# Two one-element GpSimd copies ahead of block 1's first weight sums, in a linear-attention and leaky-ReLU MLP kernel

## The chip, the core and the metric

The kernel runs on one core of one Trainium2 chip. Its time is the device time of one execution in microseconds (us). Five engines work side by side, each through its own queue of instructions in order: TensorE (PE in the profile; PEld is its weight load), VectorE (DVE), ScalarE (ACT), GpSimd (POOL) and SyncE (SP), which here only issues transfers. Engines wait for each other by semaphores.

## What is computed

Attention without softmax, with a root-mean-square norm, feeds a two-layer MLP. In float32, except that `w_in` and `w_out` reach the kernel as float64:

```python
kv = einsum('bhsd,bhse->bhde', k, v)          # batch 8, heads 8, seq 576, head 64
out = einsum('bhsd,bhde->bhse', q, kv)
x = out / sqrt(mean(out * out, -1) + 1e-6) * g_norm   # -> 4608 x 512
h = x @ w_in                                  # 512 x 2048
y = maximum(0.01 * h, h) @ w_out              # 2048 x 512
```

## The kernel before

The 4608 rows of `x` are cut into nine blocks of 512 (block 0 to 8). The 2048 columns between the two layers are cut into four chunks (`c`), each of two halves (`h`) of two tiles (`u`) of 128: sixteen tiles.

**Weights.** `w_in` and `w_out` come as 32 transfers of 64-bit numbers ("jobs"), one `w_in` and one `w_out` piece for each tile. The raw bits land in one of seven places in turn (three parts of `stage`, four of `pairs`, L209). Each job is rounded to float32 by two ScalarE instructions (L245, L247) and four VectorE instructions (L249 TENSOR_SCALAR, L253 TENSOR_SCALAR, L255 SCALAR_TENSOR_TENSOR, L258, a custom one), the last of which completes the weights. The jobs are paired crosswise (L269), so the last two are the `w_out` pieces of tile 14 and tile 15, both halves of the tile `w2_sb[1][3]`.

**Block 0** (`first_block`, L1037) runs while the weights still come. For tile n, TensorE makes `h_ps` (tile n of the hidden layer), ScalarE applies the leaky ReLU (L1055, `g`), and then TensorE adds tile n-1's product with `w_out` to four accumulators (`o_acc`). In float32 each written matmul shows as two in the trace, so both steps are groups of 8. Between the steps, `between` (L1081) loads and rounds jobs and runs block 1's attention in small steps. At the end the accumulators are copied out (L1069 ScalarE, L1071 VectorE).

**Blocks 1 to 8** use Strassen's seven products in the order 1, 2, 6, 5, 7, 3, 4 (and from block 2 a second level). For these the weights must be added up first:

- `sides_w1(c)` (L640): four GpSimd sums over a chunk of `w_in`. `sides[5]` and `sides[6]` go to `pair(0)`, `sides[7]` and `sides[3]` to `pair(1)` (`pair(i)` is the i-th quarter of `pairs`). `sides[6]` is made from `sides[5]`, `sides[3]` from `sides[6]`.
- `sides_w2(0)` (L662): four GpSimd sums over `w_out`, written to `pair(2)` and `pair(3)`.
- `combine(0, part)` (L702): eight GpSimd sums for parts 0 and 1, from `pair(0)` and `pair(1)` to `stage`, and transfers of both to DRAM by SyncE (L725 to L727), for the second level.
- `sides_x(1)` (L752): VectorE sums of block 1's `x` (`xt`, `xT`).

All such sums run through one helper, L636. An instruction that is not pinned (`pin`, L90) may be moved by the scheduler, which keeps dependences between overlapping pieces of a tile. In the built program of the kernel before, GpSimd's first sums stand as: `sides[7]`, the four sums of `w_out`, `sides[5]`, `sides[6]`, `sides[3]`, then the eight of `combine`. `sides[5]` must wait until ScalarE has read the last raw job, since that lies in `pair(0)`.

VectorE's instructions at that place stand as: the rounding of the jobs, where the last two alternate and tile 14's half is completed last; two sums for block 1's norm (L418); `xt`, `xt`, `xT` (L636); two transposes (L455); two copies of `o_acc` (L1071); a last `xt`; and `g<-h_c`, the first accumulation of block 1. TensorE's `o_acc` group of tile 14 waits for VectorE's completion of tile 14's half and for ScalarE's `g` of tile 14; the group of tile 15 waits for `g` of tile 15. The fourth product group of block 1 (product 5) waits for `g<-h_c`, which frees its bank.

Of the kernel before, what the change touches and what calls it, by code (L numbers as in the profile page):

```python
# [23 lines left out]
def kernel(  # L24
# [36 lines left out]
    nc = tc.nc  # L61
    B, H, S, D = q.shape
    DM, DF = w_in.shape
    P = 128
# [8 lines left out]
    U = 2  # L73
    NC = DF // 2 // (U * P)
# [30 lines left out]
    def view(t, lo, *shape):  # L105
        n = 1
        for d in shape:
            n *= d
        t = t[:, lo:lo + n]
        names = "abcd"[:len(shape)]  # L110
        return t.rearrange(f"p ({' '.join(names)}) -> p {' '.join(names)}",
                           **dict(zip(names, shape))) if len(shape) > 1 else t

    def pair(i, *shape):
        return view(pairs, i * NW, *shape)
# [74 lines left out]
    def make_ident():  # L190
# [9 lines left out]
    w2_sb = [[consts.tile([P, U, DM], F32, name=f"w2_{h}_{c}") for c in range(NC)]  # L200
             for h in range(2)]
# [433 lines left out]
    def add(eng, out_, a, b_, minus=False, pinned=False):  # L635
        ins = eng.tensor_tensor(out_, a, b_, op=ALU.subtract if minus else ALU.add)  # L636
        if pinned or steady:
            pin(ins)

    def sides_w1(c):  # L640


        a11, a12 = w1_sb[0][c][:, :, :2, :], w1_sb[0][c][:, :, 2:, :]
        a21, a22 = w1_sb[1][c][:, :, :2, :], w1_sb[1][c][:, :, 2:, :]
        s12 = pair(0, U, 2, 2, P)
        sides = {1: a11, 2: a12, 4: a22, 5: s12[:, :, :, 0, :], 6: s12[:, :, :, 1, :]}
        add(nc.gpsimd, sides[5], a21, a22)
        add(nc.gpsimd, sides[6], sides[5], a11, True)

        def more():  # L650
            s34 = pair(1, U, 2, 2, P)
            sides.update({7: s34[:, :, :, 0, :], 3: s34[:, :, :, 1, :]})
            add(nc.gpsimd, sides[7], a11, a21, True)
            add(nc.gpsimd, sides[3], a12, sides[6], True)
        return sides, more
# [443 lines left out]
    x_sides, _, sums, _ = sides_x(1)  # L1099
    for _ in sums:  # L1100
        pass
    h_sides, more = sides_w1(0)
    more()
    for part in range(2):
# [148 lines left out]
```

## Time and profile before

| | us |
|---|---|
| median of four runs | 917.39 (917.07 to 917.91) |
| the profiled execution | 917.91 |
| its span | 915.4 |
| outside the span | 2.5 |
| TensorE busy | 908.7 (99%) |
| VectorE busy | 634.7 (69%) |
| GpSimd busy | 367.4 (40%) |
| ScalarE busy | 327.7 (36%) |

A timeline line reads: start, duration of the group, engine, source line, operation, output<-input, partitions x elements, count; in brackets the idle time of the engine before it and what the profile takes to have ended it. All times are from the start of the span. The granted TensorE clock is 1.0 in every stretch of this profile.

### The profile page before, as it was taken

How to read it: one execution, taken by the hardware profiler on the slowest of the kernel's cores; microseconds unless marked ns; L12 is line 12 of the kernel's file. 1: busy time of each engine (PE TensorE's matmuls, PEld its weight loads, DVE VectorE, ACT ScalarE, POOL GpSimd, SP SyncE). 2: the span in 40 equal slices, each digit the busy share in tenths (PEclk: the TensorE clock that was granted, in tenths of full speed). 3: DMA queues.
4: the chain of work that ended last, by engine and by line, in shares of the span. 5: the costliest groups of instructions: out<-in, count | busy, mean ns of one | idle time of the engine just before them, and what ended most of it. 6: DMA issues, size and time to landing. Idle time of an engine off the chain costs nothing.

```text
span 915.4 us, 18027 instructions
## 1 busy us (share of the span) xinstructions
PE 908.7 (99%) x6976; PEld 775.8 (85%) x6976; DVE 634.7 (69%) x1168; ACT 327.7 (36%) x645; POOL 367.4 (40%) x438
## 2 busy tenths in 40 slices
PE   8999999999999999999999999999999999999998
PEld 5444448888998999899999999999999999999997
DVE  5876995587457876587756786678659755755565
ACT  5454433242135233533343324332343333223330
POOL 2000255977633472226321642264226422642222
PEclk9999999999999999999999999999999999999999
DMA  8999916885598779776986689757755666567632
GB/s 266 226 241 240 265 65 217 275 291 167 179 381 262 224 209 271 230 231 215 258 256 217 219 249 271 223 177 226 230 181 177 188 221 201 184 187 224 196 109 92
DMA packets 90228, 200.05 MB, mean 219 GB/s; under 512 B 9888, under 2 KB 42272, under 8 KB 90144
## 3 DMA queue, kind: packets, MB, share of 16 engines
q1 hardware_dynamic: 79680, 187.04, 68.6%
q10 hardware_dynamic: 10016, 10.69, 3.4%
q8 instruction: 55, 0.90, 0.4%
q0 software_dynamic: 448, 1.18, 0.3%
q14 instruction: 29, 0.24, 0.1%
HBM read 172.39 MB, written 26.48 MB: 217 GB/s over the span
## 4 chain that ended last, share of the span: by engine, by line
PE 96%; DVE 1%; DMA 1%; ACT 0%; issue 0%; POOL 0%; ACTq 0%; DVEq 0%; POOLq 0%
PE o_a L118 19%; PE o_c L118 18%; PE h_ha L118 11%; PE h_hb L118 11%; PE h_hc L118 8%; PE h_hd L118 8%; PE o_acc L118 6%; PE h_ps L118 6%; PE o_ps L118 3%; PE h_a L118 2%; PE h_b L118 2%; PE h_c L118 1%; PE h_d L118 1%; PE kv_ps L118 1%; DMA pairs<-in_v_dram 1%; DVE g L636 1%
## 5 line engine op out<-in xcount | busy, mean ns | idle before, releaser
L636 POOL TENSOR_TENSOR gs<-g 128x512 f32<-128x512 f32 x64 | 81.7, 1276 | 252.9 <-ACT g L832 250.9
L832 ACT ACTIVATE g<-g 128x512 f32<-128x512 f32 x124 | 78.2, 631 | 131.0 <-DVE g L636 131.0
L951 ACT COPY w_all<-h_ha 128x512 f32<-128x512 f32 x84 | 48.8, 582 | 173.9 <-PE h_ha L118 160.4
L118 PE MATMUL o_a<-pairs,gs 128*128 128x256 f32 x384 | 91.3, 381 | 0.0
L118 PE MATMUL o_c<-pairs,gs 128*128 128x256 f32 x376 | 89.2, 380 | 0.0
L636 DVE TENSOR_TENSOR o<-h_hb,o 128x128 f32<-128x128 f32 x104 | 29.8, 286 | 83.3 <-ACT pairs L951 83.2
L636 DVE TENSOR_TENSOR o<-o_c,o 128x512 f32<-128x512 f32 (+1 forms) x91 | 61.1, 672 | 23.9 <-PE o_c L118 23.6
L118 PEld LDWEIGHTS o_a<-pairs,gs 128*128 128x128 f32 x384 | 69.8, 190 | 9.2 <-POOL pairs L636 1.2
L118 PEld LDWEIGHTS o_c<-pairs,gs 128*128 128x128 f32 x376 | 68.3, 190 | 7.6
L636 DVE TENSOR_TENSOR o<-o_a,o 128x512 f32<-128x512 f32 x75 | 51.2, 683 | 28.2 <-PE o_a L118 28.1
L118 PE MATMUL h_ha<-stage,w_all 128*128 128x128 f32 x448 | 59.6, 276 | 0.0
L118 PEld LDWEIGHTS h_ha<-stage,w_all 128*128 128x128 f32 x448 | 56.6, 192 | 3.0 <-issue 0.7
L118 PE MATMUL o_acc<-w,g 128*128 128x512 f32 x128 | 57.8, 595 | 0.7 <-ACT g L1055 0.7
L118 PE MATMUL h_ps<-xT,w_all 128*128 128x512 f32 (+1 forms) x136 | 58.1, 571 | 0.3 <-DVE w_all L258 0.3
L636 POOL TENSOR_TENSOR pairs<-w_all 128x512 f32<-128x512 f32 x8 | 10.6, 1329 | 118.0 <-DMA stage<-in_moe_w_in_dram 91.3
L636 DVE TENSOR_TENSOR g<-g,pairs 128x512 f32<-128x512 f32 x84 | 55.6, 689 | 1.9
L636 POOL TENSOR_TENSOR pairs<-g 128x128 f32<-128x128 f32 x52 | 23.7, 456 | 77.3 <-PE h_hb L118 48.5
L118 PEld LDWEIGHTS o_acc<-w,g 128*128 128x128 f32 x128 | 24.0, 190 | 31.2 <-issue 29.4
L118 PEld LDWEIGHTS h_ps<-xT,w_all 128*128 128x128 f32 x136 | 25.4, 190 | 29.0 <-issue 26.3
L636 DVE TENSOR_TENSOR w_all<-h_hc,w_all 128x512 f32<-128x512 f32 x56 | 38.3, 684 | 15.9 <-PE h_hc L118 15.8
L636 DVE TENSOR_TENSOR o<-h_hd,o 128x128 f32<-128x128 f32 x78 | 22.1, 283 | 38.2 <-ACT pairs L951 38.1
L118 PE MATMUL h_hb<-stage,w_all 128*128 128x128 f32 x336 | 46.7, 275 | 0.0
(228 smaller groups left out, 2264.2 us busy)
## 6 DMA issues: line engine op xcount, KB each, us to landing
w_all<-w SPq DMA_DIRECT2D x196, 448.0 KB, 4.2
pairs<-w SPq DMA_DIRECT2D x56, 512.0 KB, 4.3
out_dram<-o ACTq DMA_DIRECT2D x35, 256.0 KB, 4.7
v_in<-in_v_dram SPq DMA_DIRECT2D x29, 288.0 KB, 5.1
k_in<-in_k_dram SPq DMA_DIRECT2D x28, 288.0 KB, 4.7
q_in<-in_q_dram SPq DMA_DIRECT2D x56, 144.0 KB, 6.3
q_in<-in_q_dram SPq DMA_DIRECT2D x56, 140.0 KB, 6.2
w<-stage SPq DMA_DIRECT2D x12, 512.0 KB, 4.4
```

Source lines behind the costliest of these rows:

```text
L118: pin(nc.tensor.matmul(*args, **kw))
L636: ins = eng.tensor_tensor(out_, a, b_, op=ALU.subtract if minus else ALU.add)
L832: nc.scalar.activation(t, t if src is None else src, func=AF.Prelu, alpha=SLOPE)
L951: nc.scalar.copy(q[:, at], bank)
```

## The change

Between the sums of `x` and `sides_w1(0)`, two GpSimd copies of one element are written:

```diff
     for _ in sums:
         pass
+    for i, r in ((1, 0), (0, 1)):
+        nc.gpsimd.tensor_copy(pair(i, U, 2, 2, P)[:1, 0, 0, r, :1], w2_sb[1][NC - 1][:1, U - 1, :1])
     h_sides, more = sides_w1(0)
     more()
     for part in range(2):
```

Each reads one element of `w2_sb[1][3][:, 1]`, the `w_out` piece of tile 15, which VectorE completes as the last but one. The first writes into the place of `sides[7]`, the second into that of `sides[6]`; those sums overwrite the element, so they come after the copy. In the built program GpSimd's order is then: the four sums of `w_out`, `sides[5]`, the two copies (the first of which waits for VectorE's completion of job 31, tile 15), `sides[6]`, `sides[7]`, `sides[3]`, the eight of `combine`. The order of the instructions on the other four engines is the same as before.

## The prediction

> **What bounds the kernel now.** I read the page's chain by engine first, then TensorE's timeline round the end of block 0, then VectorE's and GpSimd's for the same microseconds. The chain is TensorE nearly everywhere:
>
> ```profile
> PE 96%; DVE 1%; DMA 1%; ACT 0%; issue 0%; POOL 0%; ACTq 0%; DVEq 0%; POOLq 0%
> ```
>
> So only a stretch in which TensorE itself stands still can be shortened. TensorE's timeline shows one at the end of block 0:
>
> ```profile
> 122.73 3.60 PE L118 MATMUL h_ps<-xT,w_all 128*128 128x512 f32 x8
> 126.16 3.60 PE L118 MATMUL o_acc<-w,g 128*128 128x512 f32 x8
> 129.59 3.60 PE L118 MATMUL h_ps<-xT,w_all 128*128 128x512 f32 x8
> 133.91 7.10 PE L118 MATMUL o_acc<-w,g 128*128 128x512 f32 x16 [0.72 <-ACT g L1055]
> 140.85 1.89 PE L118 MATMUL h_a<-xT,w_all 128*128 128x256 f32 x8
> ```
>
> Groups of 8 start 3.43 apart (122.73, 126.16, 129.59). The next should start at 129.59 + 3.43 = 133.02; it starts at 133.91, 0.89 late. Its 16 should take 6.86; they take 140.85 - 133.91 = 6.94. Together block 1's first matmul is 0.97 later than in an unbroken stream. (The printed 0.72 counts idle time from the modelled end of the last matmul, and so less.)
>
> The bracket blames ScalarE's `g` of tile 15, which ended at 133.83. But the group that starts here is tile 14's, whose `g` ended at 126.96. What else it waits for is VectorE's half of `w2_sb[1][3]` for tile 14. Here is VectorE, a rounding undisturbed and then the last three:
>
> ```profile
> 91.61 0.42 DVE L249 TENSOR_SCALAR cut<-cut 128x512 f32<-128x512 f32 x1
> 92.06 0.43 DVE L253 TENSOR_SCALAR w<-cut 128x512 uint32<-128x512 uint32 x1
> 92.53 0.69 DVE L255 SCALAR_TENSOR_TENSOR w<-cut,w 128x512 uint32<-128x512 uint32 x1
> 93.25 0.69 DVE L258 CUSTOM_DVE_ANT_0 w<-w,add 128x1024 uint16<-128x1024 uint16 x1
> ...
> 122.92 1.49 DVE L249 TENSOR_SCALAR cut<-cut 128x512 f32<-128x512 f32 x1
> 124.34 1.75 DVE L258 CUSTOM_DVE_ANT_0 w_all<-w_all,add 128x1024 uint16<-128x1024 uint16 x1
> 126.01 1.49 DVE L249 TENSOR_SCALAR cut<-cut 128x512 f32<-128x512 f32 x1
> 127.42 1.81 DVE L253 TENSOR_SCALAR w<-cut 128x512 uint32<-128x512 uint32 x2
> 129.15 2.34 DVE L255 SCALAR_TENSOR_TENSOR w<-cut,w 128x512 uint32<-128x512 uint32 x2
> 131.42 2.34 DVE L258 CUSTOM_DVE_ANT_0 w<-w,add 128x1024 uint16<-128x1024 uint16 x2
> 133.68 1.54 DVE L418 TENSOR_TENSOR sum<-sq 128x128 f32<-128x128 f32 x2
> ```
>
> The last L258 ends at 131.42 + 2.34 = 133.76; TensorE loads its weights at 133.88. That fits VectorE as the releaser. And VectorE is slow there: L249 takes 1.49 instead of 0.42, L258 1.75 instead of 0.69. GpSimd's timeline says what is beside it:
>
> ```profile
> 122.43 1.70 POOL L636 TENSOR_TENSOR pairs<-w_all 128x512 f32<-128x512 f32 x1 [9.72 <-ACT cut L245]
> 124.21 1.33 POOL L636 TENSOR_TENSOR pairs<-pairs,w_all 128x512 f32<-128x512 f32 x1
> 125.62 1.60 POOL L636 TENSOR_TENSOR pairs<-w_all,pairs 128x512 f32<-128x512 f32 x1
> 127.17 1.78 POOL L636 TENSOR_TENSOR stage<-pairs 128x256 f32<-128x256 f32 x2
> ...
> 134.30 0.77 POOL L636 TENSOR_TENSOR stage<-pairs,stage 128x256 f32<-128x256 f32 x1
> 148.00 1.27 POOL L636 TENSOR_TENSOR pairs<-w_all 128x512 f32<-128x512 f32 x1 [12.93 <-PE h_c L118]
> ```
>
> GpSimd adds without a break from 122.43 to 135.07, just while VectorE is slow, and then idles 12.93 until TensorE frees the next place.
>
> **What the change removes.** Every sum after `sides[5]` now starts only when tile 15's half is rounded. VectorE up to the L258 at 124.34 stays as it is (`sides[5]` still runs beside it, to 124.13). From there I set undisturbed steps, from start to start in the first four lines: L249 0.45, L253 0.47, L255 0.72, L258 0.61 (93.25 to the next L249 at 93.86). So 124.34 + 0.61 + 0.45 + 2 x 0.47 + 2 x 0.72 = 127.78 is the start of tile 15's L258; it ends at 128.47 and lets GpSimd go. Tile 14's L258 starts at 128.39. Undisturbed it ends at 129.08; if the first released sum strikes it, it takes 1.75 and ends at 130.14. TensorE wants it at 133.02, its weights 0.43 earlier at 132.59. Even the later end leaves 2.4. The wait goes whole.
>
> What is late next? Tile 14's `g` (126.96) is early. Tile 15's `g` ends at 133.83 and is wanted at 133.02 + 3.43 = 136.45. So block 1 starts 0.97 earlier, and from there TensorE runs on.
>
> **What it adds.** The two copies: no row shows a GpSimd copy. The nearest are its MEMSET of 128x1, 0.10, and its sum of 128x128, 0.46. A wait can't earn time in itself, so the bounds are 0.2 and 0.9 for both; I take 0.2, since the MEMSET is as small. They lie on GpSimd alone.
>
> **What it moves on GpSimd.** Behind the waiting copy stand `sides[6]`, `sides[7]`, `sides[3]` and eight sums of `combine`. From 128.47, with copies up to 0.92, three sums at 1.33 to 1.70 and the eight at the 7.90 they took (127.17 to 135.07), GpSimd is done at 128.47 + 0.2 + 4.0 + 7.9 = 140.6, at most 142.4. Who waits?
> - TensorE wants `sides[6]` for product 6 at 144.30 - 0.97 = 143.33; it is there by 131.1. `sides[7]` and `sides[3]` come after it (products 7 and 3, at 149.06 and 150.89 in the trace before) and are there by 134.5.
> - GpSimd's own next sums wait for TensorE until 148.00 - 0.97 = 147.03. The idle 12.93 covers the delay of 5.5 to 7.3.
> - SyncE's queue stands behind these sums: the `combine` writes at 125.56 to 133.08 slide by some 6. But its next write waited anyway until 142.07, for a landing of block 0's output, and later ones for VectorE (146.75). The next loads in the queue go out at 154.04. I cost this at nothing; if the cover fails, those loads are late, with 14 us before TensorE's next `kv_ps` at 168.25.
> - `sides[7]` leaves 97.70, where it stretched an L258 to 1.75. VectorE gains 1.06 there and then waits for ScalarE at 104.51 anyway; TensorE has no wait there. Nothing.
>
> **What it moves on VectorE.** After the rounding, VectorE meets the delayed sums. From 130.14: two sums at 0.77 as now beside GpSimd; three `xt`/`xT` at 1.17, the mean of the eight `xT<-xT` rows; two transposes 2.17. That gives 130.14 + 1.54 + 3.51 + 2.17 = 137.4, earlier than now (139.24). The copies of `o_acc` then wait for TensorE, and the last `xt` is done long before `g<-h_c`. Nothing lost.
>
> The trace shows both kinds of VectorE work beside GpSimd: `xT<-xT`, read from SBUF alone, 1.17 instead of 0.68; `o<-o_c,o`, one input in PSUM, 0.68 either way. The Trainium skill, SBUF — State Buffer, section Who interferes with whom, is stricter than the first: an operation with two SBUF inputs is blocked for the whole of a GpSimd operation that reads SBUF. This speaks against the change, which only shifts the blocking from the rounding to the `xt` sums. By that rule the five sums would each wait out one GpSimd sum (an estimate: three of 1.33, two of 0.73), so VectorE would reach the end of its transposes at 140.4 instead of 137.4, and still be on time.
>
> **The sum.** 917.91 - 0.97 = 916.94 against the profiled execution (span 914.4). That execution is 0.52 above the median of the four; against the median, 917.39 - 0.97 = **916.4**, 0.1% faster. 0.2% here is 1.83 us, about what a measurement of this kernel can tell from no change, so the forecast is "within 0.2%".
>
> **Rivals.**
> - *The wait stays.* If the wait was ScalarE's `g` after all, as the bracket says, the time is 917.4. For: 133.83 lies closer to 133.91 than 133.76 does. Against: the group is tile 14's. A copy that didn't hold the sums back would end the same; but in the built order all but `sides[5]` stand behind it.
> - *VectorE becomes the bound in block 1* (slower). Product 5 starts at 146.03 and needs `g<-h_c`, which ended at 145.26; its weights load at 145.81, so 0.55 is spare. Shifted by 0.97, VectorE must begin `g<-h_c` by 143.60 + 0.55 = 144.15; every us later costs one. The price, if each of the five SBUF-only operations waits out the longest sum in view, 1.70: 130.14 + 2 x (0.28 + 1.70) + 3 x (0.69 + 1.70) + 2.17 = 143.44, plus two copies 1.38 and the last `xt` 0.69, without a further wait since GpSimd is done: 145.5. That is 1.35 late: 917.39 - 0.97 + 1.35 = 917.8. For it: eleven sums now lie over those operations. Against: the eight later sums are short (0.73 alone) and the rows beside GpSimd show 1.17, not 2.4. Beyond 0.2% it would need VectorE 2.8 late; only if the lateness also hit the next products.
> - *More comes free.* VectorE's 3.6 to 4.7 us could shorten some wait that I don't see. TensorE's waits in the whole trace add to 3.5, of which 2.8 lie before 122 us. So I price it at twice the gain, 915.5, and think little of it.
>
> **Numbers.** Forecast 0.76; the wait stays 0.10; VectorE bound 0.08 (0.03 of it within 0.2%); more 0.06. So faster by over 0.2% 0.06, within 0.76 + 0.10 + 0.03 = 0.89, slower 0.05. Range 915.6 to 917.8: it takes in no gain and the rival's price, and leaves out both tails.
>
> **What would show it.** Right: the `o_acc` groups start 3.43 apart to the end with no bracket, `h_a` starts near 139.9; L249 and L253 of the last two jobs at 0.43; GpSimd's `sides[6]` at about 128.7 and its last sum before 143; the gap before 147 still ended by TensorE. Wrong: a bracket on `o_acc` that still names `g`, or a new idle of TensorE before product 5 or 6 that names VectorE or GpSimd.

## The result, and the profile after

The changed kernel takes **916.44** us (median of 43 executions, 915.97 to 922.64), beside 917.99 for the kernel before in the same series (69 executions, 916.85 to 923.87). The ratio is 0.9987, interval 0.9982 to 0.9993: 0.6 to 1.7 us less, which is within 0.2%. The forecast was 916.4.

Single executions of either kernel end up to 7 us above their own lowest, which is more than the change is worth. So two more numbers are used below: the breaks of TensorE in a trace, and the lowest span of all executions of a kernel. (That the lowest span is the useful one I decided after seeing the medians scatter.) The lowest span is 914.3 for the changed kernel here, and 915.2 for the kernel before in each of three later series (35, 21 and 35 executions).

The profiled execution is the longest of its 43: 922.64, span 920.9. Its TensorE timeline shows why, near 91 us, long before the change does anything; the bracket is the idle time ahead of the line and its releaser:

```profile
90.92 0.33 PE L118 MATMUL kv_ps<-v_in,k_in 64*64 64x64 f32 x2
95.26 1.43 PE L118 MATMUL kv_ps<-v_in,k_in 64*64 64x64 f32 x70 [4.01 <-DMA v_in<-in_v_dram]
96.62 5.18 PE L118 MATMUL h_ps<-xT,w_all 128*128 128x512 f32 x8
101.64 3.60 PE L118 MATMUL o_acc<-w,g 128*128 128x512 f32 x8
```

TensorE waits 4.01 for a load of `v`, and the next `h_ps` takes 5.18, where the kernel before has 3.70. Before, that last `o_acc` started at 95.68: everything behind stands 5.96 later. Take this off when you compare it with the lines of before. The end of block 0 then reads:

```profile
128.69 3.60 PE L118 MATMUL h_ps<-xT,w_all 128*128 128x512 f32 x8
132.12 3.60 PE L118 MATMUL o_acc<-w,g 128*128 128x512 f32 x8
135.55 3.60 PE L118 MATMUL h_ps<-xT,w_all 128*128 128x512 f32 x8
138.99 7.03 PE L118 MATMUL o_acc<-w,g 128*128 128x512 f32 x16
145.85 1.89 PE L118 MATMUL h_a<-xT,w_all 128*128 128x256 f32 x8
```

The starts are 3.43, 3.43 and 3.44 apart, the sixteen take 145.85 - 138.99 = 6.86, and the bracket that named `g` is gone. From the `h_ps` of 135.55 to `h_a` there are 10.30; before there were 140.85 - 129.59 = 11.26. That is 0.96 less, of the 0.97 forecast. VectorE in the same stretch:

```profile
128.90 1.50 DVE L249 TENSOR_SCALAR cut<-cut 128x512 f32<-128x512 f32 x1
130.31 0.68 DVE L258 CUSTOM_DVE_ANT_0 w_all<-w_all,add 128x1024 uint16<-128x1024 uint16 x1
130.92 0.41 DVE L249 TENSOR_SCALAR cut<-cut 128x512 f32<-128x512 f32 x1
...
133.13 1.28 DVE L258 CUSTOM_DVE_ANT_0 w<-w,add 128x1024 uint16<-128x1024 uint16 x2
134.33 0.48 DVE L418 TENSOR_TENSOR sum<-sq 128x128 f32<-128x128 f32 x2
134.74 0.68 DVE L636 TENSOR_TENSOR xt<-xT 128x512 f32<-128x512 f32 x1
135.45 0.69 DVE L636 TENSOR_TENSOR xt<-xT,xt 128x512 f32<-128x512 f32 x1
136.06 1.75 DVE L636 TENSOR_TENSOR xT<-xT 128x512 f32<-128x512 f32 x1
```

Of the rounding, only the L249 that lies beside `sides[5]` is still long (1.50). The last two L258 together take 1.28, where they took 2.34. They end at 134.41, which is 5.3 before the same point of the old timeline (133.76 + 5.96). GpSimd:

```profile
128.39 1.71 POOL L636 TENSOR_TENSOR pairs<-w_all 128x512 f32<-128x512 f32 x1 [9.72 <-ACT cut L245]
133.87 1.71 POOL L1103 COPY pairs<-w 1x1 f32<-1x1 f32 x2 [3.76 <-DVE w L258]
135.66 1.61 POOL L636 TENSOR_TENSOR pairs<-pairs,w_all 128x512 f32<-128x512 f32 x1
137.23 1.72 POOL L636 TENSOR_TENSOR pairs<-w_all 128x512 f32<-128x512 f32 x1
138.91 1.28 POOL L636 TENSOR_TENSOR pairs<-w_all,pairs 128x512 f32<-128x512 f32 x1
```

It stands still for 3.76, until VectorE has completed tile 15's half, and then spends 1.71 on two copies of one element each. Compare 133.87 with VectorE's line at 133.13: two L258 in 1.28, so the first ends near 133.8, and the copies go. What stretches now is VectorE's `xT`, 1.75 beside the sum of 135.66.

### The profile page after: what moved, and what is told of

The parts are those of the page before. It is cut to its first block, busy times and chain, and to the rows that moved or that the text cites. A ratio compares the mean times of both kernels' runs of the same rounds, so it can differ in the third digit from the quotient of the medians.

```text
span 920.9 us, 18030 instructions
## 1 busy us (share of the span) xinstructions
PE 911.0 (99%) x6976; PEld 777.2 (84%) x6976; DVE 628.7 (68%) x1168; ACT 327.6 (36%) x645; POOL 367.0 (40%) x440
## 4 chain that ended last, share of the span: by engine, by line
PE 88%; DMA 11%; DVE 1%; issue 0%; ACT 0%; SPq 0%; ACTq 0%; DVEq 0%
PE o_a L118 18%; PE o_c L118 18%; PE h_ha L118 11%; PE h_hb L118 10%; PE h_hc L118 8%; PE h_hd L118 8%; DMA stage<-in_moe_w_in_dram 3%; PE o_ps L118 3%; PE o_acc L118 3%; DMA v_in<-in_v_dram 3%; PE h_ps L118 2%; DMA pairs<-in_moe_w_in_dram 2%; PE h_a L118 2%; PE h_b L118 1%; DMA q_in<-in_q_dram 1%; PE h_c L118 1%
## 5 line engine op out<-in xcount | busy, mean ns | idle before, releaser
L636 POOL TENSOR_TENSOR pairs<-w 128x512 f32<-128x512 f32 x4 | 5.3, 1330 | 104.1 <-ACT cut L245 104.1
```

## The experiments

Theory: VectorE's completion of tile 14's half was late because GpSimd's sums lay beside it; holding them back lets VectorE finish early, and that alone saves TensorE's 0.97. Rivals: it was ScalarE's `g` of tile 15 after all; or the new order of GpSimd's sums does it, and not the wait; or something else comes free. The runs, each beside the kernel before on the same chip:

| run | median us | ratio, interval | lowest span | `h_ps` to `h_a` |
|---|---|---|---|---|
| before (three series) | 918.07, 917.82, 918.23 | | 915.2, 915.2, 915.2 | 11.26 |
| e1 changed kernel again | 917.56 | 0.9990 [0.9975, 1.0005] | 914.5 | 10.30 |
| e2 copies that hold nothing | 917.82 | 0.9994 [0.9980, 1.0009] | 915.3 | 11.22 |
| e3 last two jobs swapped | 917.14 | 0.9993 [0.9977, 1.0009] | 914.7 | 10.30 |
| e4 one copy | 917.78 | 0.9998 [0.9982, 1.0014] | 914.5 | 10.30 |
| e5 hold a little longer | 916.50 | 0.9986 [0.9977, 0.9995] | 914.2 | 10.30 |
| e6 hold much longer | 924.31 | 1.0066 [1.0054, 1.0079] | 921.3 | 10.30 |
| e7 one copy, `k`, `v` first | 916.40 | 0.9984 [0.9975, 0.9993] | 914.3 | 10.30 |
| e8 e7, loads by GpSimd | 932.20 | 1.0153 [1.0139, 1.0167] | 929.8 | 10.40 |
| e9 `k`, `v` first alone | 918.04 | 0.9996 [0.9983, 1.0009] | 915.2 | 11.26 |
| e10 e3 with `k`, `v` first | 917.19 | 0.9994 [0.9982, 1.0007] | 914.6 | 10.30 |
| e11 e7 again | 916.50 | 0.9984 [0.9976, 0.9993] | 914.1 | 10.30 |
| e12 changed kernel again | 916.30 | 0.9981 [0.9973, 0.9989] | 914.2 | 10.30 |

(The last column is the distance from the last `h_ps` group's start to block 1's first `h_a`, in the profiled execution. e1 to e4 shared the first series of before, e5 to e8 the second, e9 to e12 the third.)

Of the first series every interval holds 1, although the traces differ as told below. The last two columns are the ones that tell the kernels apart.

**e1, the changed kernel again.** No edit.

> The changed kernel itself, beside the others. Theory (TensorE waited for VectorE's last L258, which GpSimd's sums held up): 0.97 us below the kernel before; from the group of tile 13 on, o_acc and h_ps start 3.43 apart without a break, and h_a follows 6.87 after the o_acc group of tile 14. The last L258 ends more than 4 us before that group. Rival (the wait was ScalarE's g, and the gain comes from somewhere else): the break of 0.9 before the o_acc group of tile 14 is still there in a profile.

Its profile, from an execution without the long wait near 91, has the unbroken stream: `h_ps` at 129.69, sixteen at 133.13, `h_a` at 139.99. What remains in it is another wait, 0.85 for `v_in` at `kv_ps` near 168, which comes back below.

**e2, copies that hold nothing.** The copies read a weight tile that was rounded long ago:

```diff
-        ... w2_sb[1][NC - 1][:1, U - 1, :1])
+        ... w2_sb[1][0][:1, U - 1, :1])
```

> The two copies stay, but read a weight tile that is rounded long before, so they hold nothing back. Theory: the sums lie over the rounding as in the kernel before, so the last L258 ends within 0.5 us of the start of tile 14's o_acc group and the break of about 0.9 is back; time that of the kernel before, +-0.3. Rival (the copies or the new order of the sums help by themselves): 0.5 to 1 us below the kernel before, with no break.

The break is back, with the old bracket. TensorE, then VectorE:

```profile
129.73 3.60 PE L118 MATMUL h_ps<-xT,w_all 128*128 128x512 f32 x8
134.01 7.11 PE L118 MATMUL o_acc<-w,g 128*128 128x512 f32 x16 [0.68 <-ACT g L1055]
140.95 1.89 PE L118 MATMUL h_a<-xT,w_all 128*128 128x256 f32 x8
```

```profile
131.52 2.34 DVE L258 CUSTOM_DVE_ANT_0 w<-w,add 128x1024 uint16<-128x1024 uint16 x2
```

The last two L258 take 2.34 as before and end at 133.86; the weights are late, and the time is that of the kernel before. So copies without that wait bring nothing. The order of the sums is not tested here: `sides[7]` runs at 97.98, ahead of the sums of `w_out`, as in the kernel before. That rival falls with e4.

**e3, the last two jobs swapped.** No copies. One line behind L269, so that tile 14's half is completed before tile 15's:

```diff
+    w_jobs[-2:] = w_jobs[:-3:-1]
```

> The kernel before, without copies; only the last two jobs change places, so that VectorE completes tile 14's half of the last w_out tile as the last but one and tile 15's as the last. GpSimd's sums lie over the rounding as before. Theory: tile 14's group then waits for the L258 that ended at 132.63 in the trace before instead of the one at 133.76. Its weights are wanted at 132.59, so the break shrinks from 0.9 to 0.1 or 0.2: 0.8 us below the kernel before. The VectorE instructions stay as long as before (L249 1.5, L258 1.2 each). Rival (it waits for ScalarE's g of tile 15, or for GpSimd): the break stays at 0.9 and the time is that of the kernel before.

Here GpSimd adds all the while and VectorE is as slow as before, but TensorE's next group needs the half that now comes first:

```profile
129.64 3.60 PE L118 MATMUL h_ps<-xT,w_all 128*128 128x512 f32 x8
133.07 7.03 PE L118 MATMUL o_acc<-w,g 128*128 128x512 f32 x16
139.94 1.89 PE L118 MATMUL h_a<-xT,w_all 128*128 128x256 f32 x8
```

```profile
131.48 2.34 DVE L258 CUSTOM_DVE_ANT_0 w<-w,add 128x1024 uint16<-128x1024 uint16 x2
```

No break, though VectorE's pair ends at 133.82 and ScalarE's `g` of tile 15 (133.28 + 0.60) at 133.88, both as late as ever. This settles the releaser: it was the one tile half, and not `g`, which the bracket of the profile before named. Of the 0.1 or 0.2 that were expected to remain, nothing is seen. Against that stands something that was not expected: 0.26 is lost again at product 6, see e10.

**e4, one copy.** Only the second copy, so only `sides[6]` and what follows from it is held; `sides[7]` goes back to its early place.

```diff
-    for i, r in ((1, 0), (0, 1)):
+    for i, r in ((0, 1),):
```

> Only the second copy (the place of sides[6]); sides[7] goes back ahead of the sums of w_out, near 97.7, where it stretches an L258 to about 1.75. Theory: the hold on sides[6] is what counts, since sides[3] and the eight sums of combine come behind it: as fast as the changed kernel within 0.2 us, 0.97 below the kernel before, and GpSimd done some 1.3 us earlier than there. Rival (moving sides[7] away from 97.7 is a part of the gain): 0.3 us or more slower than the changed kernel.

The break is gone too: `h_ps` at 130.55, sixteen at 133.98, `h_a` at 140.85. All three stand 0.85 or 0.86 later than in e1, behind a wait of 0.76 for `v_in` at `kv_ps` near 92. GpSimd's `sides[7]` and the one copy:

```profile
98.65 1.27 POOL L636 TENSOR_TENSOR pairs<-w_all 128x512 f32<-128x512 f32 x1 [92.22 <-ACT cut L245]
...
128.86 1.59 POOL L1103 COPY pairs<-w 1x1 f32<-1x1 f32 x1 [3.76 <-DVE w L258]
```

One copy does the work of two. And the sums stand here in the order of the kernel before, `sides[7]` first: the gain needs the wait, not the new order.

**e5, hold a little longer.** The copies read VectorE's `xT` sum, the fifth operation behind the last L258, so that these five meet no GpSimd sum either.

```diff
-        ... w2_sb[1][NC - 1][:1, U - 1, :1])
+        ... x_sides[7][:1, U - 1, :1])
```

> The two copies read an element of block 1's xT instead, so the sums wait 2.5 to 3 us longer, until VectorE has done the last of the sums from SBUF alone before its transposes. Theory (VectorE and GpSimd hold each other up, and only the L258 counts): the break stays away and the time is that of the changed kernel within 0.3 us; xT<-xT takes 0.68 instead of 1.75, the copies 0.2 each, GpSimd's three sums 1.27 each instead of 1.3 to 1.7, and GpSimd's last sum ends near 141, still before TensorE releases the next place at 147. Rival (the moment of the release is tuned to the microsecond, SyncE's or TensorE's next step hangs on it): 0.5 us or more slower than the changed kernel.

```profile
130.80 0.29 POOL L1103 COPY pairs<-xT 1x1 f32<-1x1 f32 x2 [6.70 <-DVE xT L636]
131.17 1.28 POOL L636 TENSOR_TENSOR pairs<-pairs,w_all 128x512 f32<-128x512 f32 x1
132.41 1.27 POOL L636 TENSOR_TENSOR pairs<-w_all 128x512 f32<-128x512 f32 x1
133.64 1.26 POOL L636 TENSOR_TENSOR pairs<-w_all,pairs 128x512 f32<-128x512 f32 x1
```

GpSimd idles 6.70 and then runs undisturbed: both copies in 0.29, where the changed kernel needs 1.71, and sums of 1.27. It ends at 139.63 + 0.73 = 140.36, in e1 at 139.78: of a hold 2.8 longer (130.80 - 128.00), 0.6 is left. VectorE's `xT` takes 0.68 and not 1.75. TensorE gains nothing more, since neither engine was its bound there any longer.

**e6, hold much longer.** The copies read the last `xt`, which VectorE makes only after it has copied `o_acc`.

```diff
-        ... w2_sb[1][NC - 1][:1, U - 1, :1])
+        ... x_sides[4][:1, U - 1, :1])
```

> The copies read block 1's last xt, which VectorE finishes at 140.6 in a profile of the changed kernel. Theory: sides[6] is done by 142.5, TensorE wants it at 143.2, so product 6 still has no wait. But the eight sums of combine end near 151 instead of 139.8: GpSimd's sums for chunk 1 start 4 us later, VectorE's eight stage sums (3.3 us now) lie beside them and stretch to 6 us or more, and SyncE's queue, which writes these sums ahead of the next loads of k and v, is 3 to 4 us late. Those loads land just in time now (issued near 162.3, wanted at 167.4), so TensorE waits 2 to 4 us at kv_ps: 2 to 4 us above the changed kernel. Rival (GpSimd's idle 7 to 13 us cover any such delay): as fast as the changed kernel.

This is 7 to 8 above the changed kernel (924.31 beside 916.44, lowest span 921.3 beside 914.3), more than expected. TensorE's waits:

```profile
154.43 1.99 PE L118 MATMUL h_a<-xt,w_all 128*128 128x256 f32 x8 [2.84 <-DVE g L636]
174.16 2.19 PE L118 MATMUL kv_ps<-v_in,k_in 64*64 64x64 f32 x70 [3.67 <-DMA v_in<-in_v_dram]
```

```profile
151.65 0.38 DVE L636 TENSOR_TENSOR stage<-w_all 128x128 f32<-128x128 f32 x1 [4.31 <-DMA w<-stage]
```

```profile
148.63 0.37 SPq L727 DMA_DIRECT2D w<-stage  x1
...
167.67 0.43 SPq L130 DMA_DIRECT2D v_in<-in_v_dram  x1
```

Two paths, both through SyncE's queue. Its writes of `combine` wait for GpSimd: the first of `stage` goes out at 148.63, in e5 at 138.33. VectorE wants that place of `stage` and stands 4.31, and TensorE waits 2.84 for the `g` behind it. This path I had not seen. And all later transfers in the queue slide: `v_in` goes out at 167.67 instead of 161.98, and TensorE waits 3.67 for it. Together 6.5 of the 7 to 8. Behind the second wait the granted clock is 0.50 from 174 to 177, and `kv_ps` and the next group take 4.40 (174.16 to 178.56) where e5 needs 3.04: 1.4 more. So the hold may not be of any length.

**e7, one copy, and `k` and `v` loaded ahead of `q`.** e4, and the loads of a pair in the other order:

```diff
-        return ("q",) if b > KV_BESIDE else ("q", "kv")
+        return ("q",) if b > KV_BESIDE else ("kv", "q")
```

> With the second copy only, and from block 2's attention on each pair's k and v loads stand ahead of its q loads in SyncE's queue. What the profiles so far show beside the break: at kv_ps near 168 TensorE finds v_in landed just in time or up to 0.9 us late (issued near 163 behind four q loads of 2.8 us). Theory: k and v are issued 2.8 us earlier, no wait at that kv_ps; 0.3 us below the second-copy kernel on the median, the other spread (a kv_ps near 91) stays. Rival (landing depends on traffic and not on the issue): no difference.

`v_in` goes out at 159.43, and `kv_ps` at 167.34 has no wait. 916.40, with 1.0 between the lowest and the highest of 11 executions, where the earlier kernels spread over 2 to 7. I took this for an effect of the early loads, and tried it alone in e9.

**e8, block 1's loads through GpSimd.** e7, and the `k` and `v` of block 1 (those that came late near 91) issued by GpSimd instead of SyncE:

```diff
+            way = nc.gpsimd if b == 1 else nc.sync
-            k_ins[b, p] = load_two(nc.sync, ...)
+            k_ins[b, p] = load_two(way, ...)
```

> As e7, and block 1's k and v loads are issued by GpSimd, which is idle from 6 to 97 us, instead of standing in SyncE's queue behind weight loads. The kv_ps near 91 waits for v_in in some executions (0.8 us in one profile, 4.0 in another). Theory: loads go out as soon as TensorE frees their place (near 70) instead of 74 to 83, the wait near 91 goes, the long executions become rare; median 0.5 to 1 us below e7. Rival: the loads then compete with weight loads, which land later and make TensorE or VectorE wait near 70 to 90: same or slower.

They go out at 11.4 and 71.4, far ahead of need, and `kv_ps` waits no more; but now other loads land late. TensorE's waits, in total, times and longest:

```profile
PE h_ps L118 <- DVE w_all L259: 5.2, 5, 2.8
PE o_ps L118 <- DVE qT L456: 4.4, 1, 4.4
```

15.8 above e7, of which these waits are 9.6; behind the two longest the granted clock is 0.50 (98 to 101 and 115.3 to 118). The DMA engines have no room in block 0 (busy shares of 0.96 to 1.1 from 85 to 95 and from 97 to 106 us in the profile after), so I read this as early `k` and `v` paid for with late weights and `q`.

**e9, `k` and `v` first, alone.** The kernel before with e7's edit of the loads and no copy.

> The kernel before, without copies, in which only the loads of k and v are written ahead of the load of q in the pairs of blocks 2 on. If the wait of TensorE on v_in near 168 is a matter of the loads' place in SyncE's queue alone, v_in is issued near 160 instead of 163 and no wait on it is left. The break at the end of block 0 is untouched: o_acc again about 0.9 late, h_a near 140.9. Time: about 1.0 above the version with both (917.4 beside 916.4), so about as the kernel before in its lowest runs plus nothing, but with a spread of about 1 us. Rival: the order of the loads itself saves time, then it comes out as low as the version with both.

No wait at `kv_ps` (169.23), although `v_in` goes out at 162.14 and not near 160 as expected; the break as before (`h_ps` 130.57, `h_a` 141.83, [0.72] on `g`), lowest span 915.2 like the kernel before, and the spread is not narrow: 916.95 to 921.07. So the early loads are worth nothing that these runs show, and my reading of e7's narrow spread falls.

**e10, swapped jobs, `k` and `v` first.** e3 with e7's edit of the loads, no copy.

> The kernel before, without copies, with the last two jobs swapped so that VectorE completes tile 14's half ahead of tile 15's, and k and v loaded ahead of q. If the 0.97 at the end of block 0 is all that the copies save, this ends where the version with a copy and early loads ended: 916.4, span 914.5, h_a near 139.9. If faster VectorE or later sums of GpSimd are worth something of their own, it ends above that; if the copies cost something elsewhere, below it.

Lowest span 914.6: 0.6 below the kernel before, and in this series 0.4 to 0.5 above the versions with a copy. The difference is one place. TensorE, VectorE and ScalarE:

```profile
141.39 1.89 PE L118 MATMUL h_c<-xT,w_all 128*128 128x256 f32 x8
143.39 1.97 PE L118 MATMUL h_a<-xt,pairs 128*128 128x256 f32 x8
```

```profile
139.04 1.27 DVE L1072 COPY o<-o_acc 128x512 f32<-128x512 f32 x2
```

```profile
139.75 0.37 ACTq L1073 DMA_DIRECT2D out_dram<-o  x1
...
142.71 0.59 ACT L858 COPY g<-h_a 128x512 f32<-128x512 f32 x1 [0.44 <-ACT o L1070]
```

Product 6 should start 1.73 behind `h_c`, at 143.12; it starts 0.27 late, just after ScalarE has emptied the bank of `h_a` (143.30). ScalarE came late to that because its queue begins with the transfer of VectorE's first copy of `o_acc`, and VectorE, still slow, reaches that copy only at 139.04. In e12, the changed kernel, VectorE makes it at 137.48:

```profile
137.48 0.69 DVE L1071 COPY o<-o_acc 128x512 f32<-128x512 f32 x1 [3.47 <-PE o_acc L118]
```

ScalarE's `g<-h_a` then starts at 142.06, and there is no delay. 0.97 - 0.27 = 0.70 is what the swap should then bring; the spans give 0.6. So a faster VectorE is worth 0.3 of its own behind the break. (Read from the order in the trace; no run took away only this.)

**e11 and e12, e7 and the changed kernel again, beside the two above.**

> One copy, and k and v loaded ahead of q, a second time, beside the two above: 916.4 as at the first time, no wait of TensorE after 27 us. It should stand 1.0 below the kernel with the early loads alone and level with the swapped jobs.

> The changed kernel as it is, beside these. Its lowest runs as those of the version with early loads (916.1 to 916.4), its median 0 to 1 above it, since v_in lands now in time and now late for kv_ps; the spread a few us instead of one.

e11: 916.50, lowest span 914.1. e12: 916.30, 914.2 and the spread 915.94 to 917.24, without any early load. Both about 1.0 below e9 by the lowest spans, 0.97 being the break. e12's spread was expected to be a few us; it is 1.3. What the spread depends on is not settled.

No version was found that is measurably below the changed kernel.

## Why the prediction was right

**What bounds.** Right. The break of 0.97 was read from the spacing of the groups rather than from the bracket (0.72), and went by 0.96. That VectorE's half of tile 14 released TensorE, against the bracket, is shown by e3.

**What the change removes.** Right in effect; VectorE is earlier still than forecast. From the start of the last struck job's L258, tile 15's L258 was to start 3.44 later; in the profile after it is 133.13 - 130.31 = 2.82, because the steps from start to start are shorter where the two jobs alternate: 0.33 for the L249 and for each L253, 0.6 for each L255, where 0.45, 0.47 and 0.72 were taken from a job rounded alone. The worse case for tile 14's half, being struck by the first released GpSimd operation (1.75), did not come: the pair takes 1.28.

**The two copies.** Mis-sized: 0.2 taken, 0.9 the upper bound, 1.71 measured. The first took 1.59 and the second 0.18 (e4's single copy 1.59). In e5, where VectorE is at its transposes meanwhile, both take 0.29. The undisturbed price was near; what failed is the bound, which left out that a copy can be held up by VectorE as a sum can. `sides[6]` came 0.9 later by it (129.60 in e12, forecast 128.7). It cost nothing, because GpSimd still idles 7.41 before its next sums (e12).

**GpSimd's delay.** Right, with errors of opposite sign. In e12 the sums end at 139.60; the forecast was 140.6. The copies were 1.5 longer and the three sums 0.5 (4.5), but the eight sums of `combine` took 5.5 instead of 7.9, since that figure had been measured beside VectorE's rounding.

**SyncE's queue at nothing.** The result was right, the cover was not. "14 us" counted from the first load in the queue to `kv_ps`. The load that TensorE waits for is a later one, `v_in`, issued at 163.05 before and wanted at 168.25: 5.2, and from issue to landing it took 4.7 there, 5.4 in e12, 6.2 in e1 and 6.9 in e5. So 0.5 was spare before, and often nothing is; `v_in` came late by 0.85 in e1 and by 1.31 in e5. The changed kernel doesn't issue it later (162.18 in e12), and that is why it cost nothing; e6 shows the price when the queue does slide.

**VectorE meets the sums.** Right in direction, too dear: of five SBUF operations forecast at lengthened durations only one is struck (`xT`, 1.75 instead of 0.68); the transposes end at 134.0 in e12, forecast 137.4. The Trainium skill, SBUF — State Buffer, section Who interferes with whom, says that whoever issues first holds the shared pair for the whole instruction and the other is blocked. That agrees here: `xT`, at 136.06, ends at 137.81, 0.54 after the end of the GpSimd sum that started before it (135.66 + 1.61 = 137.27); and the first copy is the reverse case: it starts at 133.87 and ends 1.59 later, at 135.46, when VectorE's first `xt` has ended (134.74 + 0.68 = 135.42). Why it got in only behind four VectorE operations, and not behind the first, is open.

**"And still be on time."** This sentence was wrong. By the blocking rule VectorE would have ended its transposes at 140.4, and I let that pass because I looked only at `g<-h_c` with its 0.55 of spare time. e10 shows a nearer customer: VectorE's copy of `o_acc`, the first transfer in ScalarE's queue, and the bank of `h_a` behind it. With copies starting at 139.04 product 6 was already 0.27 late; at 140.4 it would be later by the difference (an estimate: e10's timeline stands 0.23 ahead of that of before, so 140.4 - 0.23 - 139.04 = 1.1 more), and the gain of 0.97 would have been gone. The forecast of 137.4 was on the safe side of this point, the rival's price was on the wrong path.

**The rivals.** "The wait stays" is refuted by the profile after and by e3. "VectorE becomes the bound": not seen with this hold; e6's wait on `g` has VectorE in it, but through a transfer. "More comes free": the medians moved by 1.55, where the break explains 0.97; the interval of the ratio (0.6 to 1.7) holds both, and the lowest spans moved by 0.7 to 1.0. So nothing beyond the break is shown.

**The sum.** The term was right (0.97 forecast, 0.96 in the trace), but that the total came out at 916.44 beside 916.4 is luck. The four executions it starts from have a median of 917.39, the whole series has 917.99, and 0.97 off that is 917.02. The changed kernel's own median was 917.56 in e1 and 916.30 in e12.

## What to carry to other kernels

A bracket names the releaser that ended last by the profile: where two ended within 0.1 us, ask which of them this very group reads, and settle it by swapping the order of the two pieces of work. An engine with idle time ahead can be held off by a copy of one element while another engine, which shares a resource with it, finishes what the bound waits for; hold it to exactly that point, since its queue, the queue of transfers behind it and the places it frees all slide with it. And before you call a cover "14 us", take the last instruction in the queue that is needed, not the first.

## What the runs showed of the hardware

- A GpSimd copy of **one element** took 1.59 beside VectorE's rounding and sums, 0.59 and 0.64 at two other places (e2), and two took 0.29 beside VectorE's transposes (e5).
- After TensorE had stood for 4.01, the granted clock fell. Busy time by windows in the profile after (window, its length, busy time and count of PE, PEld, DVE, ACT and POOL, then PEclk, DMA share and GB/s):

```profile
91.00:95.00 4.00, 0.25 (x2) 0.11 (x2) 3.83 (x8) 1.70 (x4) 0.00 (x0) 1.00 0.96 195
95.00:97.00 2.00, 1.74 (x71) 1.65 (x72) 1.92 (x4) 0.00 (x0) 0.00 (x0) 0.81 0.68 152
97.00:102.00 5.00, 5.00 (x9) 2.08 (x9) 4.02 (x6) 0.16 (x1) 0.00 (x0) 0.74 1.01 245
102.00:106.00 4.00, 4.00 (x11) 1.78 (x10) 2.23 (x4) 1.54 (x3) 0.00 (x0) 1.00 1.10 241
```

  It was 0.81 and 0.74 in the next 2 and 5 us, and eight matmuls took 5.18 instead of 3.70: the wait of 4.01 cost 5.96 in all. The Trainium skill, TensorE: Matmul & The Clock Gate, Part 1, tells of a slower clock after an idle window of about 3.4 us. The waits of 4.01 here and of 3.67 in e6 agree with it. But in e8 the clock was 0.50 (98 to 101, eight matmuls in 5.25) after a wait of only 2.84, while after 2.84 in e6 it stayed at 1.00 (154 to 160). So the length of the wait alone doesn't decide, and what else does is not shown here.
- The time from issue to landing of one and the same load varies: 4.7 (before) to 6.9 us (e5) for the `v_in` of `kv_ps` near 168, where the kernel before had 0.5 to spare. The wait of 4.01 near 91 begins earlier: its `v_in` was issued at 86.67 (before: 81.22) and took 8.5 to land (before: 7.1). SyncE's queue was already late at the last `w_out` load ahead of it (78.04, before 72.95), while TensorE stood where it stood before (`o_acc` at 87.40 and 87.41). Up to 92 us the queue had waited 9.6 for landings of `w_out` pieces in `pairs`, before 6.0. Why those landed later, and whether this makes most of the spread, is open: e9, whose profiled execution has no wait for `v_in`, spreads as widely.
